# Feed-forward and modulation products on column groups, and key and value gradients from dense rows of all heads

## The chip, the cores and the metric

The kernel runs on one core of a Trainium2 chip. The metric is the device time of one execution in microseconds (us), lower is better. The median of 3 runs before the change is 594.23 us (593.74 to 595.05).

## The reference

One token passes through a transformer block with adaptive layer norm, and the kernel computes the block's output and its gradients. Attention is grouped-query attention over the last 4096 positions of a key and value cache. D = 1024, 32 query heads in 4 groups, head size 128, F = 3584, all in bf16.

```python
def _fwd_reference(A_x, A_k_cache, A_v_cache, A_wq, A_wo, B_x, B_w_gate, B_w_up, B_w_down, c, w_mod):
    ...
        q = (lambda x, *d: x.transpose(*d))((x @ wq).reshape(B, Sq, Hq, Dh), 0, 2, 1, 3)
        k = jnp.repeat(k_cache[:, :, Sk - W:, :], rep, axis=1)
        v = jnp.repeat(v_cache[:, :, Sk - W:, :], rep, axis=1)
        scores = jnp.einsum('bhqd,bhkd->bhqk', q, k) * Dh ** (-0.5)
        p = _softmax(scores, axis=-1)
        o = jnp.einsum('bhqk,bhkd->bhqd', p, v)
        ...
        h = _sigmoid(g) * u
        return jnp.einsum('bsf,fd->bsd', h, w_down)
    x = A_x
    mod = (_silu(c) @ w_mod).reshape(c.shape[0], 6, 1, -1)
    sa, ca, ga, sb, cb, gb = (mod[:, 0].copy(), mod[:, 1].copy(), mod[:, 2].copy(), mod[:, 3].copy(), mod[:, 4].copy(), mod[:, 5].copy())
    h = _layernorm(x, axis=-1) * (1 + ca) + sa
    x = x + ga * _A_ref(h, A_k_cache, A_v_cache, A_wq, A_wo)
    h = _layernorm(x, axis=-1) * (1 + cb) + sb
    x = x + gb * _B_ref(h, B_w_gate, B_w_up, B_w_down)
    return x
```

The outputs are the block's output and the gradients of x, both caches, wq, wo, w_gate, w_up, w_down, c and w_mod, given the gradient of the output. The cache gradients have the caches' full length, 65536 positions per group, and are zero outside the last 4096. Writing those zeros is most of what the kernel writes.

## The kernel before

A vector of 1024 is held as a column tile: 128 partitions, 8 columns. A product of such a vector with a weight matrix is made in one of two ways. In the narrow form a 128x128 block of weights is the stationary operand and one column the moving one, which gives one column of 128 results. In the wide form (`rows_mm`, L433) the column, broadcast to 32, is the stationary operand in one of four column groups of the array, and many columns of weights move past it. The result then lies in rows, 32 equal ones per group, and `rows_to_cols` (L440) picks the diagonal with a product by a mask and a reduction on DVE.

All tiles are cut from one arena by hand, and the order of all work on each engine's queue is the order of the program text. The work runs in these stages, by the time of the profile:

- Up to 25 us, the first two sections of w_mod (tiles `wm01_t[j]`, 8 of them): their products with silu(c), and `w01_fold` (L453), which transposes the shift section plus the scale section times the normalized x into `w01_T`, by two accumulated matmuls per 128x128 block. DVE makes the product in place ahead of it.
- To 84 us, transposes of k and wq, the query, the scores and the softmax. The transposed probabilities stay in `pT`.
- To 155 us, for each group a sum over key times value weighted by the probabilities (`n_ps`, L709), then to 308 us the products with wo (`b_ps`, L766), the second layer norm, and the modulation sections 2 to 5. `mod_tiles` (L384) makes the section of the second shift in narrow form, in two calls of 4 tiles.
- To 478 us, the feed-forward part in 7 blocks of 512 columns of F (the loop at L1099). `front` (L1026) makes gate and up in narrow form, `gates` (L1037) the sigmoids on ACT, `ffn_mm` (L1048) the product with w_down. `wd_ttr` and `wd_outer` make the gradients around w_down, the loop over j those of w_gate and w_up, in place in the tiles that hold the weights; then the tiles are stored and the next weights loaded. Tiles of w_gate and w_up are double-buffered; w_down has one buffer. Transposes that the end stage needs are put in between (`side`, evicted by ACT at L910).
- From 478 us, the end stage. `dwo(u)` makes an eighth of wo's gradient, `sec(j)` a part of w_mod's, `dwq_tile(j)` one of wq's, `s2(j)` the rest of w_mod's. `rebuild_P` (L1223) lays the probabilities out as rows, 8 heads at each of partitions 0, 32, 64 and 96, 4096 positions wide; `ds_chunk` (L1329) makes the score gradients in that layout; `grad_kv` (L1243) makes the value gradient dV and the key gradient dK of one group, with 4 matmuls of 8 rows per bank, evicts the banks and stores the group.

Zeros are written by `zero(n, after)` (L182), pieces of about 1 MB issued on POOL's queue, from tile `zeros` or from a region already zeroed. Where `after` is given the issue waits for that instruction, and so they are spread over the whole run by tables (`Z_N`, `Z_B`, `Z_FFN` and others), which the change leaves alone. Most loads and stores are issued on POOL's queue, those of w_down and the last few stores on SP's.

Of the kernel before, what the change touches and what calls it, by code (L numbers as in the profile page):

```python
# [59 lines left out]
def kernel(  # L60
# [323 lines left out]
    def mod_tiles(ps, tiles, ts_, first, last=KD - 1):  # L384
        for t in ts_:
            for k in range(KD):
                nc.tensor.matmul(ps[:, k:k + 1], lhsT=tiles[t][:, k * P:(k + 1) * P],
                                 rhs=cs_bf[:, t:t + 1], start=(first and t == ts_[0] and k == 0), stop=(t == last),
                                 skip_group_check=True)
# [50 lines left out]
    def rows_to_cols(out, ps, n, room=scr):  # L440
        f = room.bitcast(FP32)[:, 0:32 * n].rearrange("p (n r) -> p n r", r=32)
        tt(f, ps[:, 0:32 * n].rearrange("p (n r) -> p n r", r=32),
           mask.rearrange("p (o r) -> p o r", o=1).broadcast_to([P, n, 32]), ALU.mult)
        nc.vector.reduce_sum(out=out, in_=f, axis=AX.X)
# [8 lines left out]
    def w01_fold(j, eng):  # L453
        cols = slice(j * P, (j + 1) * P)
        for k in range(2):
            ps = new_ps("w01_ps")
            for i in range(4):
                nb = 4 * k + i
                for sct in range(2):
                    c0 = sct * D + nb * P  # L460
                    nc.tensor.matmul(ps[:, i * P:(i + 1) * P], lhsT=wm01_t[j][:, c0:c0 + P], rhs=ident_bf[:, :],  # L461
                                     start=(i == 0 and sct == 0), stop=(sct == 1), skip_group_check=True)
            o = w01_T[:, 4 * k:4 * k + 4, cols]
            v = ps.rearrange("p (n m) -> p n m", n=4)
            if eng[k] == "A":
                nc.scalar.copy(out=o, in_=v)
            else:
                cp(o, v)
# [3 lines left out]
    for j in range(KD):  # L472
        rows_mm(mod_ps, cs_bf[:, j:j + 1], heads(wm01_t[j]), j == 0, j == KD - 1)
        if j < KD - 1:
            mulv(wm01_t[j][:, D:2 * D], wm01_t[j][:, D:2 * D], b1k)
        if j > 1:
            w01_fold(j - 2, "AA")
# [11 lines left out]
    mulv(wm01_t[KD - 1][:, D:2 * D], wm01_t[KD - 1][:, D:2 * D], b1k)  # L489
    w01_fold(KD - 2, "AV")  # L490
    w01_fold(KD - 1, "AV")
# [80 lines left out]
    pT = vt([P, KT * HQ + 32], "pT", BF16)  # L572
    nc.vector.memset(pT[:, KT * HQ:], 0.0)
    p_T = pT[:, 0:KT * HQ].rearrange("p (t g h) -> p t g h", t=KT, g=G)
# [379 lines left out]
    md_ps = new_acc("md_ps")  # L954
# [3 lines left out]
    mod_tiles(md_ps, sb_t, range(4), True)  # L958
# [23 lines left out]
    mod_tiles(md_ps, sb_t, range(4, 8), False)  # L982
    cp(sb_, md_ps[:, 0:KD])
# [37 lines left out]
    fg = new_acc("fg")  # L1021
    ffn_ps = fg[:, 0:KD]
    ffn = vt([P, KD], "ffn")
    gu_t = [fg[:, 16 + 8 * i:24 + 8 * i] for i in range(2)]

    def front(q):  # L1026
        gu = gu_t[q % 2]
        for k in range(2):
            for j in range(KD):
                for i in range(4):  # L1030
                    f0 = 256 * (i // 2) + i % 2
                    col = 4 - 4 * k + i
                    nc.tensor.matmul(gu[:, col:col + 1], lhsT=ug_v[:, q % 2, j // 4, j % 4, k, f0:f0 + 255:2],  # L1033
                                     rhs=h2_bf[:, j:j + 1], start=(j == 0 and i == 0), stop=(j == KD - 1),
                                     skip_group_check=True)

    def gates(q):  # L1037
        r, gu = small[q % 2], gu_t[q % 2]
        nc.scalar.activation(out=r["sg"], in_=gu[:, 0:4], func=ACT.Sigmoid)
        nc.scalar.activation(out=r["om"], in_=gu[:, 0:4], func=ACT.Sigmoid, scale=-1.0)  # L1040

    def hh_ops(q):
        r, up = small[q % 2], gu_t[q % 2][:, 4:8]
# [4 lines left out]
    def ffn_mm(q, s):  # L1048
        for i in (2 * s, 2 * s + 1):
            for k in range(KD):  # L1050
# [374 lines left out]
```

## Time and profile before

| | before |
|---|---|
| median of the runs | 594.23 us |
| the profiled execution's own time | 594.11 us |
| its span, first to last instruction | 592.3 us |
| PE busy, matmuls | 403.6 us (68%), 4107 |
| weight loads (PEld) busy | 256.7 us (43%) |
| DVE busy | 364.3 us (62%) |
| ACT busy | 263.5 us (44%) |
| POOL busy | 156.4 us (26%) |
| mean granted clock of TensorE | 0.775 |
| HBM read, written | 78.28 MB, 185.60 MB |

The engines are PE (TensorE's matmuls), PEld (its weight loads), DVE (VectorE), ACT (ScalarE), POOL (GpSimd) and SP (SyncE); the last two mostly issue transfers here. Busy time is the union of an engine's instructions. A line such as L766 is a line of the kernel; where a helper records an operation, the line is the helper's (L233 is every tensor_tensor of DVE, L246 every tensor_scalar, L250 every multiply with sum).

The costliest groups are these (line, engine, operation, tiles, count, then busy us and mean ns):

| group | busy us | mean ns |
|---|---|---|
| L766 PE, products with wo, x494 | 116.4 | 384 |
| L233 DVE, probabilities times values, 128x2048, x64 | 76.5 | 1223 |
| L250 DVE, multiply with sum in the feed-forward part, x56 | 66.2 | 1221 |
| L709 PE, key times value, x249 | 65.2 | 378 |
| L910 ACT, eviction of transposes, x62 | 60.9 | 1015 |
| L1249 PE, dV and dK, x256 | 28.7 | 307 |
| L1033 PE, gate and up, x448 | 15.6 | 166 |

Transfers of 1 MB take 12 to 21 us from issue to landing in the median, because they stand in line behind others.

### The profile page before, as it was taken

What the parts mean: (1) busy time and instruction counts of PE and PEld (TensorE: products, weight loads), DVE (VectorE), ACT (ScalarE), POOL (GpSimd) and SP (SyncE); (2) the same over time, 40 slices, a digit from 0 to 9 for tenths busy, and PEclk for the clock granted to TensorE, in tenths of its full rate; (3) what the DMA queues carried; (4) which work ended last, traced back from release to release, by engine and by line L of the source; (5) the groups of instructions that cost most, each with busy time, mean ns of one, the idle gap of its engine ahead of it and who ended that gap; (6) DMA issues with size and microseconds to landing.
All of it is one profiled execution on the core that took longest, in us unless ns stands there. A gap on an engine that the chain in (4) does not pass through costs nothing.

```text
span 592.3 us, 10137 instructions
## 1 busy us (share of the span) xinstructions
PE 403.6 (68%) x4107; PEld 256.7 (43%) x4132; DVE 364.3 (62%) x684; ACT 263.5 (44%) x401; POOL 156.4 (26%) x258
## 2 busy tenths in 40 slices
PE   3996689999999999978866236244363455977600
PEld 2784333334344546534436225244253335656500
DVE  3765499999511020176548686687866878778740
ACT  2589514567211014212135376464655645965400
POOL 3113123212223112222221334224343145113200
PEclk9999699999999999997995567555555558755555
DMA  8999999999999999999999999999999999999998
GB/s 349 420 420 420 413 454 392 464 421 430 425 422 397 432 452 419 433 431 400 413 422 395 419 413 413 411 411 416 415 414 413 418 419 408 416 426 420 414 419 360
DMA packets 37486, 246.57 MB, mean 416 GB/s; under 512 B 6097, under 2 KB 6097, under 8 KB 23712
## 3 DMA queue, kind: packets, MB, share of 16 engines
q0 software_dynamic: 30144, 218.65, 92.3%
q1 hardware_dynamic: 7248, 27.27, 12.7%
q8 instruction: 32, 0.52, 0.3%
q14 instruction: 14, 0.11, 0.1%
q10 hardware_dynamic: 48, 0.01, 0.0%
HBM read 78.28 MB, written 185.60 MB: 446 GB/s over the span
## 4 chain that ended last, share of the span: by engine, by line
PE 38%; DMA 23%; DVE 18%; issue 9%; ACT 6%; POOL 1%; ACTq 0%; DVEq 0%; POOLq 0%; SPq 0%
PE b_ps L766 17%; DMA out_dram<-arena 13%; DVE arena L233 6%; PE n_ps L709 6%; DMA arena<-in_B_w_down_dram 5%; DVE arena L250 5%; DMA arena<-in_B_w_gate_dram 4%; DVE arena L246 3%; ACT arena L519 2%; PE t_ps L667 2%; PE tp_side L909 1%; PE tp_k L498 1%; PE w_ps L461 1%; PE ok L629 1%; PE do L1189 1%
## 5 line engine op out<-in xcount | busy, mean ns | idle before, releaser
L766 PE MATMUL b_ps<-arena 128*128 128x512 bf16 x494 | 116.4, 384 | 2.5 <-ACT arena L910 1.1
L910 ACT COPY arena<-tp_side 128x1024 bf16<-128x1024 bf16 x62 | 60.9, 1015 | 71.2 <-PE tp_side L909 71.2
L233 DVE TENSOR_TENSOR arena<-arena 128x2048 bf16<-128x2048 bf16 x64 | 76.5, 1223 | 2.3 <-PE n_ps L709 0.3
L766 PEld LDWEIGHTS <-arena 128*128 128x128 bf16 x512 | 49.3, 99 | 59.0 <-issue 5.8
L250 DVE CUSTOM_DVE_ANT_0 arena<-arena,scr 128x1024 bf16<-128x1024 bf16 x56 | 66.2, 1221 | 9.3 <-ACT scr L1072 9.3
L709 PE MATMUL n_ps<-arena 128*128 128x512 bf16 x249 | 65.2, 378 | 6.2 <-DVE arena L233 4.2
L200 POOL DMA_DIRECT2D out_dram<-out_dram x68 | 33.6, 495 | 116.0 <-PE n_ps L709 37.5
L909 PE MATMUL tp_side<-ident_bf,arena 128*128 128x128 bf16 x496 | 53.9, 285 | 12.6 <-DVE arena L233 5.3
L909 PEld LDWEIGHTS <-arena 128*128 128x128 bf16 x496 | 46.0, 132 | 18.4 <-issue 9.8
L1033 PE MATMUL fg<-h_bf,arena 128*128 128x1 bf16 x448 | 15.6, 166 | 48.6 <-DMA arena<-in_B_w_up_dram 25.5
L709 PEld LDWEIGHTS <-arena 128*128 128x128 bf16 x256 | 24.6, 97 | 41.2 <-issue 15.8
L250 DVE CUSTOM_DVE_ANT_0 arena<-arena,b1k 128x1024 bf16<-128x1024 bf16 x24 | 28.4, 1221 | 20.5 <-PE fg L1051 20.5
L281 ACT ACTIVATE arena<-scr,h 128x1024 bf16<-128x1024 bf16 x35 | 38.5, 1143 | 2.7 <-DVE dh2acc L250 2.3
L206 POOL DMA_DIRECT2D out_dram<-zeros x45 | 25.1, 561 | 55.0 <-PE q_ps L436 14.0
L942 POOL DMA_DIRECT2D out_dram<-arena x28 | 22.1, 793 | 63.0 <-ACT arena L281 43.8
L1033 PEld LDWEIGHTS <-arena 128*128 128x128 bf16 x448 | 13.9, 104 | 51.2 <-DMA arena<-in_B_w_up_dram 31.2
L1253 ACT ACTIVATE arena<-ps_kv 128x512 bf16<-128x512 f32 x48 | 26.4, 618 | 21.6 <-PE ps_kv L1249 21.6
L669 ACT CAST arena<-t_ps 128x512 bf16<-128x512 f32 x56 | 30.1, 589 | 12.1 <-PE t_ps L667 12.1
L242 DVE CAST arena<-b_ps 128x512 bf16<-128x512 f32 x6 | 4.2, 692 | 50.8 <-PE b_ps L766 50.8
L1249 PE MATMUL ps_kv<-junk,arena 8*128 8x128 bf16 x256 | 28.7, 307 | 5.6 <-DVE arena L246 5.6
L1249 PEld LDWEIGHTS <-arena 8*128 8x128 bf16 x256 | 25.2, 141 | 9.9 <-issue 9.8
L519 ACT COPY arena<-tp_wq 128x1024 bf16<-128x1024 bf16 x23 | 21.4, 1070 | 7.3 <-PE tp_wq L517 7.3
(315 smaller groups left out, 634.3 us busy)
## 6 DMA issues: line engine op xcount, KB each, us to landing
out_dram<-zeros POOLq DMA_DIRECT2D x45, 1024.0 KB, 14.0
out_dram<-arena POOLq DMA_DIRECT2D x28, 1024.0 KB, 15.4
out_dram<-arena POOLq DMA_DIRECT2D x30, 512.0 KB, 11.5
out_dram<-arena SPq DMA_DIRECT2D x20, 512.0 KB, 10.4
arena<-in_A_wq_dram POOLq DMA_DIRECT2D x8, 1024.0 KB, 20.9
arena<-in_A_wo_dram POOLq DMA_DIRECT2D x8, 1024.0 KB, 12.4
arena<-in_w_mod_dram POOLq DMA_DIRECT2D x7, 1024.0 KB, 18.6
arena<-in_B_w_up_dram POOLq DMA_DIRECT2D x14, 512.0 KB, 12.0
```

What stands on the lines that cost most here:

```text
L200: ins = nc.gpsimd.dma_start(out=as_rows(region, BIGP).bitcast(FP32), in_=zero_src[:, 0:P * ZW // 4].rearrange("i (p x) -> (i p) x", p=BIGP ...
L233: return nc.vector.tensor_tensor(out=out, in0=a, in1=b, op=op)
L250: return nc.vector.tensor_tensor_reduce(out=out, in0=w, in1=b, scale=1.0, scalar=0.0, op0=ALU.mult, op1=ALU.add, accum_out=acc)
L281: return nc.scalar.activation(out=out, in_=b, func=ACT.Copy, scale=col)
L519: nc.scalar.copy(out=blk, in_=tp[:, :])
L669: nc.scalar.copy(out=o, in_=ps)
L709: mm = nc.tensor.matmul(nbank[k][:, :], lhsT=k_nat[:, g, t_ * DH:(t_ + 1) * DH], rhs=vp[:, t_ % 2, 4 * k:4 * k + 4, :].rearrange("p h d -> ...
L766: mm = nc.tensor.matmul(bbank[p][k][:, :], lhsT=a4[:, p, h, :], rhs=wo_t[u][:, a, k * 512:(k + 1) * 512], start=(i == 0 and a == 0), stop= ...
L909: nc.tensor.transpose(tp[:, i * P:(i + 1) * P], blk[:, i * P:(i + 1) * P], ident_bf[:, :])
L910: nc.scalar.copy(out=blk if dst is None else dst, in_=tp[:, :])
L1033: nc.tensor.matmul(gu[:, col:col + 1], lhsT=ug_v[:, q % 2, j // 4, j % 4, k, f0:f0 + 255:2], rhs=h2_bf[:, j:j + 1], start=(j == 0 and i == ...
L1249: nc.tensor.matmul(ps[:, t4 * DH:(t4 + 1) * DH], lhsT=rows[32 * g:32 * g + HG, t_ * P:(t_ + 1) * P], rhs=hd[32 * g:32 * g + HG, :], start= ...
```

## The change

It has four parts.

1. In the early stage the two sections are summed on DVE (`w01_sum`: a product and an addition in place), and `w01_fold` transposes the sum with 8 transposes into one bank of bf16, evicted by one copy. Before, it took 16 matmuls into two banks of fp32 and two copies.
2. `mod_tiles`, `front` and `ffn_mm` use the wide form. Gate and up of one block come out of one set of 32 matmuls of 256 columns, and `rows_to_cols` reads them out in place in PSUM, after which that half of the bank is cleared. The feed-forward output accumulates in the other half over all blocks and is read out once, after the loop. `gates` moves from the middle of the loop over j (j == 4) to its end.
3. In the end stage the probabilities are laid out as rows of all 32 heads: a quarter of the positions at each of partitions 0, 32, 64 and 96, 1024 wide. `make_bd` makes the output gradient and the query as 128x512 tiles in which the rows of a head are zero outside its group's 128 columns. One matmul of 32 rows then makes one bank for all four groups, and `grad_kv` makes dV of all groups, then dK of all groups, each eviction writing 128 columns in each of four homes. The stores of the four groups stand behind the whole loop.
4. Around it homes in the arena are moved, and the order of the eight `dwo` becomes 2, 4, 5, 6, 7, 3, 0, 1, because the homes of dV take those of wo 4 to 7. The calls of `sec`, `dwq_tile` and `s2` are put at fixed steps of the two loops.

```diff
+    def w01_sum(j):
+        w, v = wm01_t[j][:, 0:D], wm01_t[j][:, D:2 * D]
+        mulv(v, v, b1k)
+        addv(w, w, v)
...
         if j < KD - 1:
-            mulv(wm01_t[j][:, D:2 * D], wm01_t[j][:, D:2 * D], b1k)
+            w01_sum(j)
         if j > 1:
-            w01_fold(j - 2, "AA")
+            w01_fold(j - 2, "A")
...
-    cp(sb_, md_ps[:, 0:KD])
+    rows_to_cols(sb_, md_ps, KD, md_ps)
...
+    def ffn_rows(out, col, w, stop):
+        for a in range(4):
+            nc.tensor.matmul(out[32 * a:32 * a + 32, :], lhsT=col.broadcast_to([P, 32]), rhs=w[..., 32 * a:32 * a + 32],
+                             start=False, stop=stop, tile_position=(0, 32 * a), skip_group_check=True)
...
     def front(q):
...
+        for j in range(KD):
+            w = ug_v[:, q % 2, j // 4, j % 4, :, :].rearrange("p k (s r i) -> p (k s) i r", s=2, i=2)
+            ffn_rows(gu_ps, h2_bf[:, j:j + 1], w, j == KD - 1)
 
     def gates(q):
         r, gu = small[q % 2], gu_t[q % 2]
-        nc.scalar.activation(out=r["sg"], in_=gu[:, 0:4], func=ACT.Sigmoid)
-        nc.scalar.activation(out=r["om"], in_=gu[:, 0:4], func=ACT.Sigmoid, scale=-1.0)
+        rows_to_cols(gu, gu_ps, 8, gu_ps)
+        nc.vector.memset(gu_ps, 0.0)
+        nc.scalar.activation(out=r["sg"], in_=gu[:, 4:8], func=ACT.Sigmoid)
+        nc.scalar.activation(out=r["om"], in_=gu[:, 4:8], func=ACT.Sigmoid, scale=-1.0)
...
             if more and j == 4:
                 front(q + 1)
-                gates(q + 1)
...
         if more:
+            gates(q + 1)
             hh_ops(q + 1)
...
     assert not jobs
+    rows_to_cols(ffn, ffn_ps, KD, ffn_ps)
...
+    def make_bd(out, col):
+        tp = new_tp("tp_bd")
+        for tc_ in range(4):
+            nc.tensor.transpose(tp[32 * tc_:32 * tc_ + 32, 0:P], col, ident_bf[:, :], tile_position=(0, 32 * tc_))
+        tt(out.rearrange("p (g d) -> p g d", g=G),
+           tp[:, 0:P].rearrange("p (o d) -> p o d", o=1).broadcast_to([P, G, P]),
+           in_group.rearrange("p (g o) -> p g o", o=1).broadcast_to([P, G, P]), ALU.mult)
...
+    def grad_kv(rows, bd, scale, home, engs, between=lambda t_: None):
+        for t_ in range(KT):
+            between(t_)
...
+            nc.tensor.matmul(ps[:, :], lhsT=rows[r, t8 * P:(t8 + 1) * P], rhs=bd[r, :], start=True, stop=True,
+                             tile_position=(32 * tc_, 0))
+            o, v = home[:, :, t_ * P:(t_ + 1) * P], ps.rearrange("p (g d) -> p g d", g=G)
+            if engs[t_ % len(engs)] == "A":
+                nc.scalar.activation(out=o, in_=v, func=ACT.Copy, scale=float(scale))
             else:
-                ts(o, ps[:, :], float(scale), ALU.mult)
...
+                ts(o, v, float(scale), ALU.mult)
...
-    for u in range(4):
+    for u in (2, 4, 5, 6):
         dwo(u)
...
+    def dv_between(t_):
+        if t_ == 8:
+            sec(4)
+            dwq_tile(0)
+        elif t_ == 16:
+            sec(5)
+            dwq_tile(1)
+        elif t_ == 24:
+            sec(6)
+            dwq_tile(2)
+
+    grad_kv(P_b2, DO_bd, 1.0, dv_home, "A", dv_between)
+    for g in range(3):
+        kv_store(out_3, dv_home, g)
...
+    def dk_between(t_):
+        if t_ == 4:
+            dwq_tile(4)
+            s2(0)
+            s2(1)
+        elif t_ == 10:
+            dwq_tile(5)
+            s2(2, tail)
+            s2(3, tail)
+        elif t_ in (18, 25):
+            g = (t_ - 4) // 7
+            dwq_tile(4 + g, tail)
+            s2(2 * g, tail)
+            s2(2 * g + 1, tail)
+
+    grad_kv(dS, Q_bd, SCALE, dk_home, "AV", dk_between)
+    for g in range(G):
+        kv_store(out_2, dk_home, g, nc.gpsimd if g < 2 else tail)
```

## The prediction

> **What bounds the kernel now.** I read the page's slices first, then busy time by stage, then the POOL timeline where transfers are issued late, then the timelines of the engines at the places that the diff touches.
>
> ```profile
> DMA  8999999999999999999999999999999999999998
> GB/s 349 420 420 420 413 454 392 464 421 430 425 422 397 432 452 419 433 431 400 413 422 395 419 413 413 411 411 416 415 414 413 418 419 408 416 426 420 414 419 360
> DMA packets 37486, 246.57 MB, mean 416 GB/s; under 512 B 6097, under 2 KB 6097, under 8 KB 23712
> ...
> q8 instruction: 32, 0.52, 0.3%
> ```
> ```profile
> 8.00:52.00 44.00, 39.09 (x602) 31.32 (x602) 26.74 (x52) 28.64 (x40) 9.93 (x20) 1.00 1.02 420
> 52.00:84.00 32.00, 22.09 (x183) 11.18 (x185) 20.90 (x46) 17.96 (x46) 7.17 (x13) 0.84 1.13 419
> 84.00:315.00 231.00, 210.90 (x1401) 103.14 (x1423) 121.58 (x171) 71.30 (x127) 56.23 (x99) 0.98 1.04 424
> 315.00:480.00 165.00, 68.15 (x1026) 59.96 (x1026) 121.83 (x260) 94.62 (x105) 55.75 (x80) 0.53 1.12 415
> 480.00:505.00 25.00, 18.26 (x291) 13.94 (x292) 20.36 (x59) 10.54 (x16) 11.88 (x17) 0.77 1.11 411
> ```
> The slices say that the 16 DMA engines are busy all the time, 9 of 10 or more in 38 of 40 slices, the first and last being the edges. In the second fence (us, then PE, PEld, DVE, ACT, POOL busy, granted clock, DMA share, GB/s) the share is over 1 in every stage, because packets of two queues overlap, while no compute engine is full in all of them. 246.57 MB at 416 GB/s are 592.7 us, which is the span (592.3). Counting the packets in flight in the trace, I find at least 14 on 16 engines at every moment from 4 us to 588 us. So the kernel is bound by bytes, and an engine matters only where it lets the queue of issued transfers run dry. I therefore counted bytes issued minus bytes landed (sizes at the issue, packets at their end). The smallest stocks are 1.33 MB at 67 us and 1.46 MB at 495 us; 1.7 MB at 92 us; about 2 MB in the feed-forward stage; 2.4 MB and more after 505 us, up to the last issue. At 420 GB/s 1.33 MB last 3.2 us, 1.46 MB 3.5 us.
>
> ```profile
> 66.45 2.15 POOL L206 DMA_DIRECT2D out_dram<-zeros  x4 [7.69 <-DVE rsum L590]
> ...
> 494.73 0.88 POOL L1221 DMA_DIRECT2D out_dram<-arena  x1 [1.91 <-DVE arena L246]
> 497.17 0.54 POOL L1221 DMA_DIRECT2D out_dram<-arena  x1 [1.55 <-DMA out_dram<-zeros]
> ```
> The two low points differ. At 66.45 POOL waits 7.69 us for the softmax's reciprocal: compute is late. At 494.73 the page names DVE, but DVE finished that tile at 486.9 (its sixteen L246 began at 485.25, 0.41 us each): POOL was waiting for earlier transfers to land, as in the next line, and compute has 7.8 us in hand.
>
> **The change, part by part.**
>
> *Early fold.* Per tile j it takes out 8 of 16 matmuls and one of two ACT evictions and adds one DVE addition.
> ```profile
> 15.29 0.40 PE L436 MATMUL mod_ps<-arena,cs_bf 128*32 128x512 bf16 x4
> 15.62 1.07 PE L461 MATMUL w_ps<-ident_bf,arena 128*128 128x128 bf16 x16
> 16.62 0.40 PE L436 MATMUL mod_ps<-arena,cs_bf 128*32 128x512 bf16 x4
> ...
> 13.06 1.90 DVE L233 TENSOR_TENSOR arena<-arena,b1k 128x1024 bf16<-128x1024 bf16 x3 [2.58 <-DMA arena<-in_w_mod_dram]
> ```
> PE's 1.33 us per tile becomes 0.40 + 0.53. DVE's multiply costs 0.63 us back to back (1.90 for 3); the addition has the same shape and type but both operands in the arena, so 0.63, bounded by 0.42 (the 128x1024 copy of L242 into scr) and 1.22 (twice the elements, L233). Two make 1.26 us per tile: DVE becomes the pace. Seven from 13.06 end at 21.9, where the page has the next step (L233 from mod_ps) at 21.06; the eighth tile's addition then delays its fold by another 0.6. Less the one eviction saved, the k transposes start about 1.2 us later than 24.79 (0 to 4 by the bounds). The next 40 us are a chain of PE, DVE and ACT, so the zeros at 66.45 go out at 67.65. What hides it is the stock of 3.2 us, less the time from an issue to its first packet. The shortest I find is 1.15 us (the load issued 91.40 to 92.21). Cover 2.0, delay 1.2: cost 0, up to 2 at the upper bound.
>
> *Second modulation products (mod_tiles).* 64 narrow matmuls become 32 of 256 columns, the shape of mod_rows (64 in 2.1 us): a wash. Reading them out needs 0.42 + 0.42 us (the 128x256 rows of L233 and L444) for a copy of 0.17: +0.7 us on DVE at 289 us, where 5 MB are queued. Cost 0.
>
> *Feed-forward.* Seven blocks of about 24 us. Front: 64 narrow matmuls become 32 of 256 columns. After the last load lands 44 narrow ones run now (1.33 us); then 16 wide ones, 0.5 us at full clock by mod_rows and 1.0 at the half clock of this stage (granted 0.53); the stride of 2 elements in the moving operand is in no row, and I bound it at 1.0 and 2.0 and take 1.0. The product ffn_mm goes from 16 narrow (0.59) to 8 wide (about 0.5). DVE gains 0.42 + 0.42 for the read-out and about 0.3 for clearing 256 columns, and loses the addition of 0.16: +1.0 us a block. The sigmoids now stand behind three side evictions on ACT (1.0 each), so the gate can come up to 3 us later.
> ```profile
> 383.18 0.16 DVE L233 TENSOR_TENSOR hh_bf<-sg,fg 128x4 bf16<-128x4 f32 x1 [4.26 <-ACT om L1040]
> ...
> 386.09 1.23 DVE L250 CUSTOM_DVE_ANT_0 arena<-arena,b1k 128x1024 bf16<-128x1024 bf16 x1 [2.49 <-PE fg L1051]
> ...
> 409.29 1.23 DVE L250 CUSTOM_DVE_ANT_0 arena<-arena,b1k 128x1024 bf16<-128x1024 bf16 x1 [4.09 <-PE fg L1051]
> ```
> Here DVE idles 4.26 + 2.49 us in one block and 4.09 in the next, waiting for loads. Behind the delayed gate on DVE stand wd_ttr, wd_outer and the store of w_down. The buffers turn once in two blocks (store 10 us, load 10 to 12 us, compute 24), and a longer compute leg only shortens the time that transfers stand in line: 1 to 3 us of the 20. Cost 0; if that cover were gone, 1 to 3 us in each of 6 blocks.
>
> *End of the feed-forward.* rows_to_cols(ffn) (0.84) now precedes the reduction of dh2, and op_ps, which shares its bank, moves behind it: it ran at 468.4, 32 matmuls in 1.4 us, and DVE now waits for it before dln2. About +2.4 us on the chain to dattn; the cover is the 7.8 us of the first dwo store. Reordering dwo adds nothing: tiles 4 to 6 need do4[1], done at 487.4, before DVE has finished tile 2. Cost 0.
>
> *End stage.* The evictions stay 32 for dV (ACT) and 32 for dK; PE loses 192 of 256 matmuls of L1249 and 96 of 128 of L1228; ACT loses 3 of 4 rebuild_P copies (0.95 each); DVE 6 of 8 stt (0.75) but pays two broadcast products of 128x512 (0.69 each by its 128x512 rows; bounds 0.42 and 1.22). An eviction now writes four pieces of 128 columns: 0.50 to 0.60 us now, 1.0 at most (twice). dV takes 32 x 0.50 = 16 us on ACT from about 518, ending at 534 (before: 541). Its stores leave together at 534 to 536 where they left at 523, 529, 535 and 541; but sec(4) to sec(6) and dwq 0 to 2, six transfers of 1 MB, no longer queue behind them on POOL and leave by 530. So the stock at 534 stays near 4 MB. Then dK: DVE has 16 x 0.62 + 4 x 1.2 (dwq) + 8 x 0.66 (s2) = 20 us, plus some 3 for s2(3), whose buffer waits for sec(7) to land, as now (3.24 us at 559.11); compute ends near 570, as now (570.9). The four dK stores (4.2 MB, 10 us) leave last, two on POOL's queue and two on SP's. That starves nothing as long as compute ends before 591 - 10 = 581 us. Cost 0, and 5 us if evictions took 1.0 us.
>
> *Instructions.* Some 720 matmuls and as many weight loads fewer, of 10137: 14% of the 0.52 MB that q8 fetches, 0.07 MB, -0.2 us.
>
> The sum against the profiled execution: 594.11 (span 592.3 and 1.8 around it) - 0.2 + 0.2 for a shaved stock at 67 us = 594.1. It lies 0.12 under the median of 594.23.
>
> [...] The early fold makes PE wait for DVE, 0.93 us of work in 1.26. The granted clock reads 1.00 from 10 to 60 us with PE nearly full, 0.53 in the feed-forward stage, and 1.00 at 300 to 310 us where PE was busy 7.43 of 10. So at a share of 0.74 it held. [...]
>
> **Rivals.**
> 1. *Slower: the early stage runs the queue dry at 67 us.* If PE stays at half clock to 26 us, a tile costs 2 x 0.93 = 1.9 us, 0.6 over DVE's pace: 8 x 0.6 = 4.8, but for one tile's worth; with part of the k transposes (4.63 us) at half speed, the zeros come about 5 us later. Over the cover of 2.0: 3 us, 597. It decides from a delay of 2 us on. For: the least stock of the run, behind compute. Against: 1.00 at a share of 0.74. Chance 0.15.
> 2. *Slower: the feed-forward loop becomes compute-bound.* 6 blocks x 1 to 1.5 us: 600 to 603. For: two of its buffers turn on landings and the gate moves behind side work. Against: 4 to 7 us of DVE idle per block. Chance 0.07.
> 3. *Slower: late stores in the end stage.* Strided evictions of 1.0 us would end dV at 550, with the stock gone near 545: about 5 us, 599. Against: the stored bytes that move ahead. Chance 0.05.
> 4. *Faster: DMA works better with less going on.* The feed-forward stage moves 415 GB/s and 480 to 505 us 411, where 420 is seen elsewhere: at 420 they would save 165 x 0.012 + 25 x 0.021 = 2.5 us, 591.6. For: nothing but the difference. Against: 420 GB/s at 8 to 52 us, with PE and weight loads the fullest of all. Chance 0.13.
>
> **Chances.** No change by my sum: 0.60, own range 593.0 to 595.4. Within 0.2% (1.2 us) is what a measurement of this kernel can't tell from nothing, as its runs lie 593.74 to 595.05. Faster 0.13 (rival 4), slower 0.27 (1 to 3). 0.8 of it lies from 592.2 to 598: the low end takes in part of rival 4, the high end rival 1.
>
> **What would show it.** DMA share stays at 9 in every slice but the edges and GB/s at 415 to 424: right. An empty stretch near 68 us, and GB/s under 400 in that slice: rival 1. The first k transposes (L498) at 26 us: the early step's size. Block period at 24 to 25 us, DVE's waits for loads shorter by 1 to 3 us: feed-forward right. Compute ending between 565 and 575 us with 15 to 25 us of transfers behind it: end stage right. A share under 1 anywhere between 10 and 585 us would make me wrong.

## The result and the profile after

The changed kernel takes 596.34 us (median of 6 runs, 596.03 to 597.28) against 594.47 us for the kernel before (6 runs beside them, 593.74 to 595.05). The ratio is 1.0037, with a 95% interval of 1.0027 to 1.0048: slower by 1.9 us, more than the 0.2% that was to count as no change. The profiled execution spans 594.6 us (596.4 with what lies around it); before it was 592.3.

The page of the changed kernel, the lines that answer to those shown of before (DMA share in tenths and GB/s in 40 slices, the packets):

```profile
DMA  9999999999999999999999999999999999999998
GB/s 348 421 420 421 397 459 349 464 429 429 432 424 382 426 456 433 420 429 393 428 415 395 418 417 415 411 415 420 411 415 414 421 414 408 421 420 423 416 414 338
DMA packets 37481, 246.48 MB, mean 415 GB/s; under 512 B 6097, under 2 KB 6097, under 8 KB 23712
```

The bytes are 0.09 MB fewer (0.07 forecast), so the lost time must be time in which the DMA engines moved less. The digits don't show it: a slice of 15 us with 2 us missing is still a 9. The GB/s line does. Slice 5 (59 to 74 us) fell from 413 to 397 and slice 7 (89 to 104 us) from 392 to 349; after that only the last slice, where the run ends, falls by as much (360 to 338). The same for three stages and then in short windows (us, then PE, PEld, DVE, ACT, POOL busy, granted clock, DMA share, GB/s):

```profile
52.00:84.00 32.00, 22.25 (x203) 11.80 (x202) 20.73 (x47) 20.99 (x50) 8.65 (x15) 0.79 1.10 410
84.00:315.00 231.00, 210.60 (x1294) 100.85 (x1319) 122.44 (x167) 70.49 (x125) 56.70 (x100) 0.98 1.03 422
315.00:480.00 165.00, 64.70 (x748) 47.80 (x740) 129.63 (x271) 92.77 (x106) 54.62 (x78) 0.61 1.10 415
```
```profile
27.00:30.00 3.00, 3.00 (x33) 3.00 (x31) 2.68 (x6) 0.00 (x0) 0.53 (x1) 0.51 1.02 426
...
68.00:72.00 4.00, 3.06 (x26) 2.06 (x27) 1.83 (x7) 1.56 (x6) 2.15 (x4) 0.50 0.95 359
94.00:98.00 4.00, 3.16 (x15) 1.28 (x14) 3.97 (x6) 0.00 (x0) 1.17 (x2) 1.00 0.55 162
```

The last two windows in the kernel before:

```profile
68.00:72.00 4.00, 3.76 (x36) 1.40 (x40) 3.58 (x7) 3.28 (x16) 0.61 (x2) 0.50 1.10 420
94.00:98.00 4.00, 3.89 (x19) 1.66 (x17) 3.87 (x4) 2.16 (x4) 2.32 (x4) 1.00 1.12 439
```

Two stretches run short: 359 GB/s at 68 to 72 us (420 before) and 162 GB/s at 94 to 98 us, at a DMA share of 0.55 (439 and 1.12 before). The view books a packet where it starts, and the packets at 94 us are of 64 KB and take 2.4 us each, so it exaggerates there: spread over the time that the packets took, the changed kernel moves 353 and 310 GB/s in the two windows, the one before 408 and 405. Packets in flight, counted in the traces, show it most directly. The kernel before has 15 or more at every moment from 4 to 588 us on the 16 engines. The changed one falls to 6 at 69.6 to 70.7 us and again to 6 at 95.1 to 96.2. The feed-forward stage moves 415 GB/s, as before, and the stage behind it 412 (before 411). The first of the short windows shows something else: at 27 to 30 us the granted clock is half, with PE full. Counted in landed bytes, the changed kernel is 0.57 us late at 30 MB (about 75 us), 2.3 us at 40 MB (about 101 us) and 1.58 us at 240 MB. So up to 240 MB nothing more was lost after 101 us; the run's end adds another 0.5, which is taken up below.

The timeline of PE in the changed kernel, around the eighth tile of the early fold (start, duration, then in brackets the idle time ahead and what ended it), then the k transposes of the kernel before:

```profile
22.27 0.62 PE L455 MATMUL tp_w<-ident_bf,arena 128*128 128x128 bf16 x8 [0.44 <-DVE arena L233]
25.72 0.62 PE L455 MATMUL tp_w<-ident_bf,arena 128*128 128x128 bf16 x8 [2.83 <-DVE arena L233]
26.18 6.26 PE L496 MATMUL tp_k<-ident_bf,arena 128*128 128x128 bf16 x80
```
```profile
24.79 4.63 PE L498 MATMUL tp_k<-ident_bf,arena 128*128 128x128 bf16 x80
```

PE stands still for 2.83 us before the eighth tile's fold. That tile's sum is queued on DVE behind the read-out of mod_ps (22.13 to 24.26 us), and its product and addition end at 25.7. Then come the 80 k transposes, which start at 26.18 (before: 24.79, so 1.39 later) and take 6.26 us in place of 4.63, because a stretch of 3.41 us (27.1 to 30.5) runs at half clock. 1.39 + 1.63 = 3.02 us, and that is by how much the zeros are late, in POOL's timeline (the third line is of the kernel before):

```profile
69.47 2.15 POOL L206 DMA_DIRECT2D out_dram<-zeros  x4 [6.97 <-DVE rsum L587]
...
93.86 0.81 POOL L378 DMA_DIRECT2D arena<-in_A_wo_dram  x1 [3.02 <-PE g_ps L433]
```
```profile
91.40 0.81 POOL L378 DMA_DIRECT2D arena<-in_A_wo_dram  x1 [3.02 <-PE g_ps L436]
```

66.45 became 69.47. The second line is the transfer at the other short stretch: a load of wo that POOL issues when the g_ps product is done. It went out at 91.40 before, so it is 2.46 us late.

### The profile page after: what moved, and what is told of

Same layout as the page of the kernel before. It is cut to its first block, busy times and chain, and to the rows that moved or that the text cites. A ratio compares the mean times of both kernels' runs of the same rounds, so it can differ in the third digit from the quotient of the medians.

```text
span 594.6 us, 8679 instructions
## 1 busy us (share of the span) xinstructions
PE 392.2 (66%) x3388; PEld 222.0 (37%) x3412; DVE 374.8 (63%) x702; ACT 258.9 (44%) x391; POOL 156.9 (26%) x258
## 4 chain that ended last, share of the span: by engine, by line
PE 40%; DVE 23%; DMA 19%; ACT 7%; issue 6%; POOL 1%; ACTq 0%; DVEq 0%; POOLq 0%; SPq 0%
PE b_ps L763 16%; DMA out_dram<-arena 9%; DVE arena L233 7%; DMA arena<-in_B_w_gate_dram 6%; PE n_ps L706 6%; DVE arena L250 6%; DVE arena L246 4%; DMA arena<-in_B_w_down_dram 3%; ACT arena L517 2%; PE t_ps L664 2%; PE ps_kv L1245 2%; PE tp_k L496 2%; PE tp_side L906 1%; PE bc_ps L337 1%; PE do L1182 1%
## 5 line engine op out<-in xcount | busy, mean ns | idle before, releaser
L233 DVE TENSOR_TENSOR arena<-arena 128x2048 bf16<-128x2048 bf16 (+1 forms) x72 | 82.0, 1164 | 2.5 <-PE n_ps L706 0.3
L763 PEld LDWEIGHTS <-arena 128*128 128x128 bf16 x512 | 49.2, 99 | 59.2 <-issue 6.0
L906 PE MATMUL tp_side<-ident_bf,arena 128*128 128x128 bf16 x496 | 52.0, 278 | 15.3 <-DVE arena L233 6.4
L906 PEld LDWEIGHTS <-arena 128*128 128x128 bf16 x496 | 44.2, 129 | 25.6 <-issue 15.9
L1026 PE MATMUL fg<-arena,h_bf 128*32 128x256 bf16 x224 | 14.2, 410 | 45.6 <-DMA arena<-in_B_w_gate_dram 45.6
L706 PEld LDWEIGHTS <-arena 128*128 128x128 bf16 x256 | 24.6, 97 | 41.3 <-issue 15.8
L1249 ACT ACTIVATE arena<-ps_kv 128x512 bf16<-128x512 f32 x48 | 25.0, 723 | 26.7 <-PE ps_kv L1245 26.7
L1245 PE MATMUL ps_kv<-arena 32*128 32x512 bf16 x64 | 24.4, 559 | 17.1 <-DVE arena L246 16.6
L1026 PEld LDWEIGHTS <-h_bf 128*32 128x32 bf16 x224 | 6.9, 128 | 51.1 <-DMA arena<-in_B_w_gate_dram 42.1
L246 DVE TENSOR_SCALAR arena<-arena,cs_col 128x4096 bf16<-128x4096 bf16 (+1 forms) x16 | 16.0, 1014 | 10.3 <-DMA out_dram<-arena 10.2
```

The source lines that it names most:

```text
L233: return nc.vector.tensor_tensor(out=out, in0=a, in1=b, op=op)
L246: return nc.vector.tensor_scalar(out=out, in0=a, scalar1=s1, scalar2=None, op0=op0)
L706: mm = nc.tensor.matmul(nbank[k][:, :], lhsT=k_nat[:, g, t_ * DH:(t_ + 1) * DH], rhs=vp[:, t_ % 2, 4 * k:4 * k + 4, :].rearrange("p h d -> ...
L763: mm = nc.tensor.matmul(bbank[p][k][:, :], lhsT=a4[:, p, h, :], rhs=wo_t[u][:, a, k * 512:(k + 1) * 512], start=(i == 0 and a == 0), stop= ...
L906: nc.tensor.transpose(tp[:, i * P:(i + 1) * P], blk[:, i * P:(i + 1) * P], ident_bf[:, :])
L1245: nc.tensor.matmul(ps[:, :], lhsT=rows[r, t8 * P:(t8 + 1) * P], rhs=bd[r, :], start=True, stop=True, tile_position=(32 * tc_, 0))
```

## The experiments

First, which part of the change loses the time. Undo the early fold alone (the products that add the two halves on PE come back, the rest of the change stays):

```diff
 def w01_fold(j, eng):
-    tp = new_tp("tp_w01")
-    for nb in range(KD):
-        nc.tensor.transpose(tp[...], wm01_t[j][...], ident_bf[:, :])
+    for k in range(2):
+        ps = new_ps("w01_ps")
+        for i in range(4):
+            for sct in range(2):
+                nc.tensor.matmul(ps[...], lhsT=wm01_t[j][:, c0:c0 + P], rhs=ident_bf[:, :], ...)
...
-            w01_sum(j)
+            mulv(wm01_t[j][:, D:2 * D], wm01_t[j][:, D:2 * D], b1k)
```

> The changed kernel with the early fold of before (16 matmuls and two evictions per tile, no addition on DVE). Theory A, two places: the early stage ran the DMA queue dry at 69 to 71 and 95 to 98 us and cost about 1.5 us, and the last stores cost about 0.8 us more, so 595.0 (594.7 to 595.3), zeros after the softmax issued near 66.5 us instead of 69.47, no moment under 14 packets in flight between 60 and 100 us. Theory C, all of it early: 594.4. Theory B, the cost sits in the feed-forward or end stage: 596.3.

Measured: 594.40 us (593.90 to 595.07, 11 runs), ratio to before 1.0004 [0.9996, 1.0013]. Its windows at the two short stretches:

```profile
68.00:72.00 4.00, 3.42 (x64) 1.61 (x64) 3.89 (x8) 3.29 (x16) 1.07 (x3) 1.00 1.09 415
94.00:98.00 4.00, 3.95 (x20) 1.75 (x19) 3.79 (x4) 3.35 (x7) 2.86 (x5) 1.00 0.99 395
```

Neither is short, and at least 16 packets are in flight from 60 to 110 us. Feed-forward, modulation products, end stage and tail together cost nothing that can be measured. The counterpart, the early fold alone put into the kernel before:

```diff
-            mulv(wm01_t[j][:, D:2 * D], wm01_t[j][:, D:2 * D], b1k)
+            w01_sum(j)
...
-            w01_fold(j - 2, "AA")
+            w01_fold(j - 2, "A")
```

> The kernel before with the new early fold alone. Theory A: 595.9 (595.6 to 596.2), zeros at 69.5 us, packets in flight down to 6 or so near 70 us, end of the span as before. Theory C: 596.4. Theory B: 594.5.

Measured: 596.09 us (594.61 to 597.48, 10 runs), ratio 1.0030 [1.0020, 1.0040]. The k transposes start at 26.20 and take 6.26 us, the zeros go out at 69.50. The runs spread over 3 us, so the median can't tell theory A from C, but the cost that A puts on the last stores did not show with the fold undone. By both medians the loss is the early fold's, whole (1.86 us here, 0.17 without the fold).

Next, which half of the 3.02 us decides: the 1.39 that DVE's additions cost, or the 1.63 of half clock. The changed kernel with PE kept at work in the gap, by 40 transposes that nothing reads:

```diff
     w01_sum(KD - 1)
     w01_fold(KD - 2, "A")
+    tp_idle = new_tp("tp_idle")
+    for i in range(40):
+        nc.tensor.transpose(tp_idle[:, (i % KD) * P:(i % KD + 1) * P], ident_bf[:, :], ident_bf[:, :])
     w01_fold(KD - 1, "V")
```

> The changed kernel with 40 transposes of the identity, whose result nobody reads, in the 2.83 us in which PE waits for the last addition. If half of the 3.0 us of delay is the lower clock after that wait, the 80 transposes of k take 4.6 us again instead of 6.26, the zeros go out near 67.9 us, and the time is 595.0 to 595.8. If the transposes of k were late for another reason, 6.26 us stay and the time is 596.3.

Measured: 594.76 us (594.01 to 595.58, 11 runs), ratio 1.0010 [1.0001, 1.0018]. PE's timeline in this kernel:

```profile
22.72 2.40 PE L491 MATMUL tp_idle<-ident_bf 128*128 128x128 bf16 x40
25.72 0.62 PE L455 MATMUL tp_w<-ident_bf,arena 128*128 128x128 bf16 x8 [0.60 <-DVE arena L233]
26.18 4.63 PE L499 MATMUL tp_k<-ident_bf,arena 128*128 128x128 bf16 x80
```

The k transposes start at the same 26.18, but 80 of them take 4.63 us again. The zeros go out at 67.85, 1.40 us late instead of 3.02, and most of the loss is gone: 0.53 us against the kernel before beside it, in place of 1.87, a little under the range expected. Work that nobody needs made the kernel faster. It moved a second thing, which I saw only later: the clock also came back earlier at the o/kB sums behind the softmax (64 matmuls of the probabilities with values and keys: 3.64 us, 5.39 in the changed kernel), and what follows them was early.

Then I tried to put bytes into the low point. The changed kernel with one transfer of zeros moved from behind the softmax to before it:

```diff
-Z_Q = [0] * 6 + [1, 3]
+Z_Q = [0] * 6 + [2, 3]
...
-Z_B = [n + (i in (31, 38)) for i, n in enumerate(spread(29, 43))] + ...
+Z_B = [n + (i in (38,)) for i, n in enumerate(spread(29, 43))] + ...
```

> The changed kernel with one zero piece of 1 MB issued at 51 us in place of one near 190 us, the rest of the order alone; compute stays as late as in the changed kernel. Theory A: the stock at 70 us is 1 MB higher, no drop of packets in flight at 69 to 71 us, 594.8 to 595.3. If lateness costs by itself, through the chain of compute and not through an empty queue: 596.3.

Measured: 596.86 us (595.69 to 597.51, 5 runs), ratio 1.0044 [1.0032, 1.0056]: the expectation missed. A window of this kernel:

```profile
330.00:340.00 10.00, 4.07 (x40) 2.90 (x40) 9.43 (x21) 5.51 (x9) 5.19 (x8) 0.51 0.98 369
```

The two early dips are filled (15 or more packets in flight throughout), but a new one stands at 330 to 340 us (369; the changed kernel has 411 there), with 9 packets in flight at the least. In landed bytes this execution is level with the kernel before at 138 MB (329 us) and 1.2 us late at 144 MB (344 us). The compute is still 3 us late, with its first feed-forward product at 314.74 against 311.38 before, and the transfer that filled the early dip is missing later. Shifting a transfer only moved the place where lateness is paid. The profiled execution was the fastest of the five (595.69 us); where the others lost more isn't on record.

Is it lateness as such? The kernel before, with two, and with five, unread products of 128x1024 on DVE ahead of the last tile's:

```diff
+    for _ in range(2):      # 5 in the second kernel
+        mulv(scr, b1k, b1k)
     mulv(wm01_t[KD - 1][:, D:2 * D], wm01_t[KD - 1][:, D:2 * D], b1k)
```

> The kernel before with 2 multiplications of 128x1024 on DVE (0.63 us each) that compute nothing used, between the query's input and the last tile's product. Theory L, compute that is late by d at the zeros after the softmax costs d less a cover of about 2 us, whatever made it late: d is 1.3 us if the clock holds through the longer wait of PE (2.3 us), and the time stays at 594.2 to 594.5; if the clock falls, d is 2.9 and the time 595.1 to 595.6. Rival, the loss hangs on the new fold's instructions themselves: 594.2 in any case.

> The same with 5 such multiplications, 3.2 us, PE waiting 4.2 us. Theory L: the clock falls, d is 4.5 to 5.0 us, the zeros go out at 71 to 71.5 us, the queue runs dry near 70 us, and the time is 596.7 to 597.4. Rival: 594.2.

Measured: 596.68 us (594.98 to 597.96, 6 runs), ratio 1.0036 [1.0022, 1.0051], with two; 598.79 us (597.53 to 600.2, 5 runs), ratio 1.0079 [1.0065, 1.0093], with five. Nothing of the change is in them, and the loss is there. PE and POOL in the first, then PE in the second:

```profile
26.57 1.01 PE L461 MATMUL w_ps<-ident_bf,arena 128*128 128x128 bf16 x15 [2.30 <-DVE arena L233]
27.42 4.63 PE L500 MATMUL tp_k<-ident_bf,arena 128*128 128x128 bf16 x80
...
69.09 2.15 POOL L206 DMA_DIRECT2D out_dram<-zeros  x4 [6.98 <-DVE rsum L592]
```
```profile
28.21 1.78 PE L461 MATMUL w_ps<-ident_bf,arena 128*128 128x128 bf16 x15 [4.48 <-DVE arena L233]
```

The first missed its expectation too. The gap of 2.30 us leaves the clock full (80 transposes in 4.63 us), yet the zeros are 2.64 us late where 1.3 had been expected: the other 1.3 came ahead of the products, since the clock was first granted in full at 17.8 us and not at 14.9, and mod_ps was done at 22.3 in place of 21.0. And by theory L a delay of 2.64 would cost 0.6, not 2.4. In the second, after the gap of 4.48 us, the 80 transposes take 6.64 us, and the zeros are 7.02 us late. It missed upward as well: with 7 us even the zeros behind q_ps, at 50 to 60 us, came too late (294 GB/s in that window, 422 before).

Can the fold keep its fewer matmuls without the gap? The changed kernel, with sums and folds of tiles 6 and 7 moved behind the first k transposes, where PE has other work while DVE adds:

```diff
-        if j < KD - 1:
+        if j < KD - 2:
             w01_sum(j)
...
-    w01_sum(KD - 1)
-    w01_fold(KD - 2, "A")
-    w01_fold(KD - 1, "V")
...
     for j in range(KD):
+        if j == 2:
+            w01_sum(KD - 2)
+            w01_sum(KD - 1)
+            w01_fold(KD - 2, "V")
+            w01_fold(KD - 1, "V")
```

> The changed kernel with the sums and folds of tiles 6 and 7 moved behind the first 12 transposes of k, so that PE has work while DVE adds. All else as in the changed kernel. If the wait of PE and the clock after it are the cause: the transposes of k start near 22 us and run at full clock, the zeros go out between 66.2 and 67.8 us, and the time is 594.0 to 594.6. If DVE's added 5 us delay the query in any order: zeros at 69 us or later, 596.3.

Measured: 594.51 us (594.24 to 596.23, 11 runs), ratio 1.0010 [1.0001, 1.0019]. The zeros go out at 67.18, 0.73 us late. The loss is mostly gone, and nothing is gained over the kernel before, as it must be where bytes bound the run. Eight of the 11 runs lie between 594.24 and 594.67, three between 596.09 and 596.23. The same kernel, with the last dK stores all on SP's queue:

```diff
-        kv_store(out_2, dk_home, g, nc.gpsimd if g < 2 else tail)
+        kv_store(out_2, dk_home, g, tail)
```

> The kernel e8_folds_behind_k with all four dK stores on SP's queue. In the changed kernel 8.65 us lie between the 244th MB and the end of the span, in the one before 8.11. If the stores on two queues cause that, this is 0.4 to 0.6 us under e8_folds_behind_k; if not, the same.

Measured: 594.78 us (594.11 to 596.74, 11 runs), ratio 1.0017 [1.0006, 1.0028]. No gain: the order of the last stores isn't the matter. From 244 MB landed to the end the kernel before takes 8.11 us and the changed one 8.65, but the kernels with two and with five products, whose tail is that of before, take 8.58 and 8.76. This small difference comes and goes without the change.

Last, at which of the two low points is the time lost? Up to here I had held the zeros at 69.5 us to be the place (theory F). But most of the late bytes appear at 94 to 98 us (theory S). The changed kernel, with unread transposes in the softmax's waits, so that the clock is full for the o/kB sums behind it: the zeros stay late, the load of wo does not.

```diff
+    tp_idle = pacc.tile([P, 1024], BF16, name="tp_idle", tag="acc")
+    def idle_mm(n):
+        for i in range(n):
+            nc.tensor.transpose(tp_idle[:, (i % KD) * P:(i % KD + 1) * P], ident_bf[:, :], ident_bf[:, :])
+    idle_mm(32)
     for tb in range(4):
...
         tps.append(tp)
+        idle_mm(4)
```

> The changed kernel with 48 unread transposes of the identity placed where PE waits for the softmax's exponentials (61.9 to 65.5 us, 3.52 us idle), so that the granted clock, 0.50 from 66 to 74 us there, comes back before the o/kB sums (64 matmuls, 5.39 us at half clock, 3.64 at full in the early-fold-undone kernel). The zeros behind the reciprocal stay 3.0 us later than before (69.4 to 69.5), while the first load of wo, 2.46 us late in the changed kernel (93.86 against 91.40), comes 1.5 to 2 us sooner, 0.4 to 1 late. Theory F (the loss is made at the first low point, the zeros at 69.5): loss stays, 595.9 to 596.7. Theory S (the loss is made at the second low point, 92 to 98 us, by the delay of the first wo load; the first point costs 0.6 at most): 594.5 to 595.3. If the clock doesn't come back sooner, nothing is told apart: 596.3.

And the kernel before, with the zeros on time and what follows late:

```diff
     zero(Z_SM, last)
+    for _ in range(4):
+        mulv(scr, b1k, b1k)
```

> The kernel before with four unread DVE products of 128x1024 (0.63 each, 2.5 us) between the softmax's reciprocal and the scaling of p, so that the zeros leave on time (66.4 to 66.6) and only what comes behind them is late: the first load of wo at 93.9 in place of 91.40. Theory F: 594.3, no change. Theory S: a loss of the size that the changed kernel shows, 1.6 to 2.4 us: 595.9 to 596.7, with GB/s under 250 between 94 and 98 us and no dip between 66 and 72.

Measured: 595.22 us (594.33 to 595.92, 11 runs), ratio 1.0017 [1.0008, 1.0026], and 595.24 us (594.78 to 596.44, 11 runs), ratio 1.0019 [1.0010, 1.0028]. POOL's timeline of the first, then its windows; then the same of the second:

```profile
69.54 2.16 POOL L206 DMA_DIRECT2D out_dram<-zeros  x4 [6.97 <-DVE rsum L595]
...
91.72 0.81 POOL L378 DMA_DIRECT2D arena<-in_A_wo_dram  x1 [3.02 <-PE g_ps L433]
```
```profile
68.00:72.00 4.00, 2.87 (x50) 1.96 (x51) 2.22 (x9) 2.00 (x8) 2.16 (x4) 1.00 0.95 364
...
94.00:98.00 4.00, 3.89 (x19) 1.72 (x18) 3.93 (x4) 1.85 (x4) 2.01 (x3) 1.00 0.92 354
```
```profile
66.98 2.16 POOL L206 DMA_DIRECT2D out_dram<-zeros  x4 [6.97 <-DVE rsum L590]
...
92.89 0.81 POOL L378 DMA_DIRECT2D arena<-in_A_wo_dram  x1 [3.02 <-PE g_ps L436]
```
```profile
68.00:72.00 4.00, 1.64 (x24) 0.79 (x28) 3.80 (x9) 1.66 (x9) 1.14 (x3) 0.90 1.11 419
...
94.00:98.00 4.00, 3.18 (x15) 1.36 (x15) 4.00 (x4) 0.88 (x2) 1.04 (x3) 1.00 0.91 311
```

In the first the zeros are 3.09 us late and the load 0.32; 68 to 72 us is short (364 GB/s), and it loses 1.1 us. At 94 to 98 the view reads 354, but packets in flight never fall under 16 there; they fall to 5 at 69.7 to 70.8. In the second the zeros are 0.53 late and the load 1.49 (I had expected 2.5; the o/kB sums started 2.12 us late and took 5.32 us in place of 5.95); 68 to 72 is full, 94 to 98 short, and it loses 1.1 us too; packets in flight fall to 9 at 94.2 to 94.8 and nowhere earlier. In landed bytes the first is 0.59 us late at 30 MB, the second 0.02 at 30 MB and 1.13 at 40 MB. So theory F is out. The first kernel's time lies in the range of S, whose limit of 0.6 for the first point is about what the bytes show there; the second lies under it, its load having come less late. Each point loses time of its own. All kernels together, against the kernel before run beside them:

| kernel | zeros late, us | wo load late, us | median lost, us | lost by the profiled execution, us |
|---|---|---|---|---|
| changed | 3.02 | 2.46 | 1.87 | 1.93 |
| early fold alone | 3.05 | 2.11 | 1.86 | 1.72 |
| before, two products | 2.64 | 2.73 | 2.40 | 2.32 |
| before, five products | 7.02 | 6.21 | 4.51 | 5.92 |
| busy in softmax | 3.09 | 0.32 | 1.08 | 0.79 |
| second point late | 0.53 | 1.49 | 1.10 | 0.82 |
| PE kept busy | 1.40 | -0.92 | 0.53 | 0.03 |
| folds behind k | 0.73 | 0.32 | 0.23 | 0.39 |
| folds and tail | 1.04 | -1.69 | 0.50 | 0.07 |
| early fold undone | 0.46 | -1.97 | 0.17 | 0.01 |
| one transfer of zeros ahead | 3.01 | 2.13 | 2.63 | 1.46 |

The delays are those of one profiled execution each, so its own loss, in the last column, is what they have to explain. They fit one sum, made afterwards with two fitted covers: the loss is the larger of (zeros late less 2.0) and (wo load late less 0.4). It gives 2.1 for the changed kernel, 1.7, 2.3, 5.8, 1.1 and 1.1 for the next five, and nothing for the four behind them; the last row, where bytes were moved, is not of this kind. That it is the larger and not the sum would follow if time lost at the first point isn't lost again at the second, the transfers being late by then as well; no run here shows that by itself.

## Why the prediction was wrong

The step that failed is the *Early fold*, "Cover 2.0, delay 1.2: cost 0", and what happened is its first rival by place and nearly by price (597 forecast for it, 596.3 measured), though by another route. That the price comes so near is in part luck: the rival put the delay at 5 us, where it was 3.0, and the whole loss at 67 us, where landed bytes put 0.57 of it. In place of the step the runs show a delay of 3.02 us, 1.63 of it from half clock, that outlasts the cover at two low points and costs 1.9 us.

**The delay was mis-sized.** DVE's pace was right: fourteen products of 0.66 us from 12.8 us end at 22.2 (predicted: 21.9), and the k transposes start 1.39 us later (predicted: 1.2). But their duration was taken over from the kernel before, and half clock added 1.63 us, so that the zeros came at 69.47 where I had put 67.65. (The sum did hold 0.2 us "for a shaved stock at 67 us"; the bytes there were 0.57 late.) I weighed the clock by a mean share (0.93 us of PE in 1.26) and reasoned that "at a share of 0.74 it held". What decided was one gap, 2.83 us long, which stood in my own terms: the eighth tile's sum comes behind the read-out of mod_ps on DVE, and PE has nothing queued before it. I counted that gap as delay, 0.6 us, and not as idle time that the clock sees. The PE-kept-busy kernel shows it: same start, full clock for the k transposes, most of the loss gone.

The release of the clock, which the rival put at 26 us, did come later: the record of the granted clock begins at full at 14.9 us in the kernel before (the fold's 16 matmuls take 1.62 us from 13.74 and 1.07 from 15.62 on) and at 20.2 in the changed one. The 1.00 that the prediction reads "from 10 to 60 us" holds only from 14.9 on, since the view prints 1.00 where there is no record; in the changed kernel the 8 transposes of a tile take 1.03 us up to 20 us and 0.62 after. But this cost nothing here. PE needed 1.51 us per tile at half clock, and DVE ended its fourteen products at 22.2 all the same; the PE-kept-busy kernel, at full from 17.5 on, starts the k transposes at the same 26.18.

In the record of the granted clock of the kernel before and of the changed one, every stretch at full or half but the last is a multiple of 3.413 us (3.413, 6.827, 10.240, 27.307, and so on). So the granted clock changed here only at the edges of windows of that length, and what tells the kernels apart is PE's work in one window. The window that ended with the drop, 23.65 to 27.06 us, held 1.34 us of matmuls, those from 25.72 on. In the kernel with two products the window of the gap, 24.67 to 28.08, held 1.50 us, and the clock stayed at full.

**The cover was looked for at one place only.** For the zeros at 67 us the 2.0 was about right: the four kernels with no bytes moved whose zeros are 2.64 to 3.09 us late are 0.28 to 0.59 us late in landed bytes at 30 MB, which makes the cover 2.4 to 2.5. (Its term of 1.15 us is not that of the load named there, whose first packet started 2.44 us behind the issue, the engines being busy; but the zeros of the changed kernel, issued to empty engines, took 1.13.) But the prediction names a second low point, "1.7 MB at 92 us", and gives it no cover of its own. By the same arithmetic it would have had 1.7 MB / 420 GB/s less 1.15, about 2.9 us; the fit to the runs gives about 0.4. The packets in the trace of before show where most of the difference lies. A packet counts as outstanding until it ends, and the last 16 packets ahead of the wo load, one on each engine as I take them, are of 64 KB, 1.05 MB together. These end one after the other, from 93.89 to 95.80 us. The load was issued at 91.40, and in the changed kernel, where engines stood empty, its first packet started 1.52 us behind the issue. So, as an estimate, the first engine had 93.89 - 91.40 - 1.52 = 1.0 us to spare and only the last one 2.9. Why the fit gives 0.4 and not 1.0 stays open.

A DMA share under 1 in a window, which the prediction names as the sign of being wrong, could not have told: the kernel before itself reads 0.76 at 98 to 102 us, with 15 or more packets in flight all the time. Nor does a share over 1 need the two queues that the prediction names: at 52 to 84 us of the kernel before the packets of q0 alone make up 1.12, with up to 27 in flight.

**Where the mechanism was right.** The feed-forward block costs about what was forecast and all of it lies in DVE's idle time:

```profile
381.86 1.05 PE L1026 MATMUL fg<-arena,h_bf 128*32 128x256 bf16 x16 [2.59 <-DMA arena<-in_B_w_gate_dram]
```
```profile
386.98 0.16 DVE L233 TENSOR_TENSOR hh_bf<-sg,gb_rest 128x4 bf16<-128x4 f32 x1 [2.74 <-ACT sg L1038]
...
410.48 1.22 DVE L250 CUSTOM_DVE_ANT_0 arena<-arena,b1k 128x1024 bf16<-128x1024 bf16 x1 [0.76 <-PE fg L1026]
```

In this block of the changed kernel, the last 16 wide matmuls take 1.05 us (predicted 1.0 without a cost for the stride of two elements), the read-out 0.43 + 0.42 + 0.27 (predicted 0.42 + 0.42 + 0.3), the gate comes 3.80 us later (386.98 for 383.18), of which 1.85 is how late the whole run is by then in landed bytes, so about 2 (predicted up to 3), and DVE's wait for the next load falls from 4.09 to 0.76 us. The cover is nearly used up, not exceeded, and rival 2 did not happen. op_ps moved from 468.4 to 482.0, and DVE's first product of dwo from 485.25 to 488.00 in the kernel with the early fold undone, 2.75 us (predicted 2.4) where 7.8 were in hand. In the changed kernel it starts at 490.66, and the first dwo store goes out at 496.20 for 494.73, 1.5 us later, no more than the whole run is late: no short stretch there. The end stage:

```profile
519.01 15.79 ACT L1249 ACTIVATE arena<-ps_kv 128x512 bf16<-128x512 f32 x32 [0.83 <-PE ps_kv L1245]
```
```profile
562.54 0.75 DVE L246 TENSOR_SCALAR arena<-arena,cs_col 128x2048 bf16<-128x2048 bf16 x1 [10.22 <-DMA out_dram<-arena]
```

32 evictions take 15.79 us (predicted 16; no cost of the four pieces shows), so rival 3 fell. The wait for sec(7)'s landing was 10.22 us where I had "some 3", and compute ended near 575 and not 570. That cost nothing either, the limit being 581. Rival 4 (415 GB/s rising to 420 with less going on) did not happen: 415 in the feed-forward stage in both. The instructions fetched fell by 0.09 MB (0.52 to 0.43; predicted 0.07), worth 0.2 us, which the loss hides.

What the prediction said would show rival 1, an empty stretch near 68 us and GB/s under 400 in that slice, is there (397, and 6 packets in flight at 69.6 to 70.7 us); the DMA digit, also named, is not a view that can show 2 us.

## What to carry to other kernels

Where a kernel is bound by bytes, list every low point of the queue with the cover of each, and run a delay past all of them: here each of two points whose cover it exceeded lost time, and bytes put into them moved the bill to a third. Take the cover from the time at which the first engine runs out of packets, not from the stock as a whole: with one 64 KB packet left on each engine the two were, by the estimate above, 1.0 and 2.9 us. Where an edit takes work off PE, look for the longest single gap that it leaves, not for the mean share: 2.83 us of waiting cost 1.63 us more in the half-clock stretch that followed. Before thinning PE out, place other PE work (here the k transposes) into the gap, or leave the spare matmuls in.

## What the runs showed of the hardware that I had not expected

Of windows of 3.41 us in a stretch at full clock, those with 0.75 us (busy in softmax, 23.12 to 26.53), 1.05 us (changed kernel, 54.4 to 57.8) and 1.34 us of matmuls (changed kernel, 23.65 to 27.06) were followed by half clock, and one with 1.50 us (two products, 24.67 to 28.08) was not. In the traces of the kernel before and the changed one, up to 480 us, all 15 full-clock windows with up to 1.34 us of matmuls were followed by half clock, all 150 with 2.00 us or more by full, and of the ten between, with 1.46 to 1.79 us, four by half and six by full. The edges lie elsewhere from kernel to kernel (one at 14.94 us before, one at 20.23 in the changed kernel, 1.55 windows apart), so the same gap can fall into one window or be shared by two. And busy time is not the whole measure: in the kernel before the window from 509.87 us holds 3.23 us of matmuls, over half of it 64 narrow ones with 2 moving columns, and half clock follows at 513.28.

The clock's release moves from kernel to kernel: full from 14.9 us before, from 17.8 with two products, from 20.2 in the changed kernel. The same 64 matmuls of the o/kB sums took 3.64 us in four kernels and 5.01 (early fold alone) to 5.95 (before) in six others, by where in them the clock came back: 3.6 us behind the start of the first with 5.39 us (changed kernel, full from 74.85), 4.7 with 5.95 (before, full from 72.96). Kernels near the edge of their cover scatter accordingly: 594.61 to 597.48 for the early fold alone and two groups 1.4 us apart for the folds behind k, while 49 runs of the kernel before, beside these, all lie between 593.67 and 594.84. That the clock's phase makes the two groups is argued from this, not shown, since each kernel left one trace.
